# Wider squares, one of them on ScalarE, another load order and earlier softmax chains in a fused attention and channel-mix kernel

## The chip, the core and the metric

The kernel runs on one core of a Trainium2 chip. The metric is the device time of one execution in microseconds. TensorE (PE) multiplies matrices and writes to PSUM; VectorE (DVE) and ScalarE (ACT) do elementwise work; GpSimd (POOL) here mostly issues the DMAs that convert f32 to bf16 on the way; SyncE (SP) issues the other DMAs and the DMA transposes. Each engine works through its own list of instructions in order and waits on semaphores for the others.

## The reference

Two layers follow each other, for 4 batches of 6208 rows and 256 channels. The first is an attention over channels: a 256 x 256 matrix per batch, built from q and k normalised over the rows, goes through a softmax and multiplies v. The second mixes each row with the row before it and runs a two-matrix network with a squared relu and a gate.

```python
qn = q / (np.linalg.norm(q, axis=1, keepdims=True) + 1e-06)
kn = k / (np.linalg.norm(k, axis=1, keepdims=True) + 1e-06)
s = kn.transpose(0, 2, 1) @ qn / tau
a = softmax(s)                        # with the usual maximum subtracted
x = v @ a                             # [4, 6208, 256]
xk = mu_k * x + (1.0 - mu_k) * x_prev # x_prev: the row before, zeros in front
xr = mu_r * x + (1.0 - mu_r) * x_prev
k = np.maximum(xk @ w_k, 0.0)         # 1024 wide
out = sigmoid(xr @ w_r) * (k * k @ w_v)
```

## The kernel before

**Blocks.** A batch has 12 blocks of 512 rows and 64 left-over rows; the left-over rows of all batches make one last block. The main loop has an index i over blocks and eight steps j = 0 to 7 in each. At iteration i it holds three blocks in flight. For block i + 2, `x_half` makes x transposed from v (steps 0 and 2), `mix_delta` (step 3) and `mix` to xk (steps 4 and 5) follow on VectorE. For block i + 1, `up` makes one of eight 128-wide slices of the hidden layer in each step (PSUM tile kT_ps, three buffers), ScalarE applies the relu into kr, and `square` squares two slices at a time on VectorE into kk, a step after the second relu; the mix to xr runs at steps 0 and 2. For block i, `down` multiplies kk with w_v and xr with w_r (PSUM tile vr_ps, two buffers), `finish` takes the tanh on ScalarE and the last product on VectorE, and a DMA on SP stores the result. The last square of block i (`square(i, 7)`) is placed at step 0 of iteration i, and `down(i, 1)` at step 2 is the first that reads it.

**The next batch's covariance.** Batch 0's q and k are loaded, cast and multiplied ahead of the loop (VectorE casts, ScalarE squares). For batches 1 to 3 the covariance is cut into units, one per 128 rows: 1 for the left-over rows and 48 for the twelve groups of 512 rows. `unit` is put into the loop at the steps named in `slots`: three units in iteration 0, five in iteration 1, six in iterations 2 to 7, and three to five afterwards. Five early units are multiplied in iteration -1. A unit is two matmuls into s_ps (one buffer for batches 1 to 3). `feed` keeps ScalarE two units ahead with the squares of q and k, two units in one instruction, and `next_add` adds these squares to the accumulator acc on VectorE: at steps 1, 6 and 7, two steps or more after the square, and at every step once the batch's softmax chain is under way.

**The softmax chain.** When a batch's last unit is placed, `softmax_pieces` gives a list of pieces, and each following step of the loop takes one from its front: copy s_ps out (evac), fold acc, sum over partitions (norms), copy and take the root on GpSimd (roots, roots2), invert, spread the factors with a matmul, scale, exp, weigh. `None` is a step without a piece. `FOLD` is the length of the list at which fold is in front; it stays there while adds of that batch are open. The pieces norms and spread each take a PSUM buffer with the tag xT_ps, of which there are two, shared with x_half. weigh writes a_sb, which the first `x_half` of the next batch reads: x_half(12) at iteration 10, x_half(24) at 22, x_half(36) at 34.

**Loads.** GpSimd issues in program order v(0), w_k, q and k of the left-over rows, v(1), q and k of group 1, w_r, w_v, v(2), q and k of group 2; then v(i + 5) at step 0 of each iteration, and q and k up to three groups ahead of the unit in hand (`loads_upto`), into five buffers. v(0), v(1) and v(2) are transposed on TensorE, the others by DMA on SP, issued at step 5 of iteration i for block i + 4. The tile qk holds [128 partitions, 4 rows, q or k, 256 channels], so each row of q lands as 512 bytes between rows of k.

Of the kernel before, what the change touches and what calls it, by code (L numbers as in the profile page):

```python
# [10 lines left out]
F32 = mybir.dt.float32  # L11
BF16 = mybir.dt.bfloat16
AX = mybir.AxisListType.X
AF = mybir.ActivationFunctionType
OP = mybir.AluOpType
# [3 lines left out]
def kernel(  # L19
# [13 lines left out]
    nc = tc.nc  # L33
    B, N, C = q.shape
    D = C
    DF = moe_w_k.shape[1]
    P = 128
    M = 512
    S = M // P
    assert C == 256 and DF == 1024  # L40
    NB = N // M
    L = N - NB * M
# [3 lines left out]
    bounded = abs(inv_tau) < 32.0  # L46

    const = ctx.enter_context(tc.tile_pool(name="const", bufs=1))
    pq = ctx.enter_context(tc.tile_pool(name="pq", bufs=4))
    pn = ctx.enter_context(tc.tile_pool(name="pn", bufs=2))  # L50
    p2 = ctx.enter_context(tc.tile_pool(name="p2", bufs=3))
# [35 lines left out]
    sums = {}  # L87
# [5 lines left out]
    def sizes(b):  # L93
        return [1] + [S] * (NB - 1) + ([S // 2] * 2 if b == 0 else [S])

    def order(b):
        g = list(range(len(sizes(b))))
        return [1, 2, 0] + g[3:] if b == 0 else g

    def rows_of(b, g):  # L100
        return (P if g else L), sizes(b)[g]

    def qk_src(t, b, g):
        if g == 0:
            return t[b, NB * M:, :].rearrange("(p j) c -> p j c", j=1)
        r = P * sum(sizes(b)[1:g])
        n = sizes(b)[g]
        return t[b, r:r + P * n, :].rearrange("(p j) c -> p j c", p=P)

    def group_load(b, g):  # L110
        rows, n = rows_of(b, g)
        qk = pq.tile([P, S, 2, C], BF16, name="qk", tag="qk", bufs=5)
        groups[b, g] = (qk,)
        if b == 0:
            qk2 = pq.tile([P, S, 2, C], BF16, name="qk2", tag="qk2", bufs=4)
            groups[b, g] += (qk2,)
            t_f = []
            for i, t in enumerate((q, k)):
                f = pq.tile([P, S, C], F32, name=f"f{i}", tag=f"f{i}", bufs=6)
                nc.sync.dma_start(f[:rows, :n], qk_src(t, b, g))  # L120
                t_f.append(f)
            groups[b, g] += tuple(t_f)
        else:
            for i, t in enumerate((q, k)):
                nc.gpsimd.dma_start(qk[:rows, :n, i, :], qk_src(t, b, g))  # L125

    def group_cast(b, g):
        rows, n = rows_of(b, g)
        qk, qk2, *t_f = groups[b, g]
        for i in range(2):  # L130
            nc.vector.tensor_copy(qk[:rows, :n, i, :], t_f[i][:rows, :n])  # L131
        for i in range(2):
            nc.scalar.activation(qk2[:rows, :n, i, :], t_f[i][:rows, :n], AF.Square)  # L133

    def unit_square(b, g, s):

        rows, n = rows_of(b, g)
        if s % 2:
            return
        qk = groups[b, g][0]  # L140
        if n == 1:
            t = pq.tile([P, 1, 2 * C], BF16, name="sq", tag="sq1", bufs=2)
            sums[b, "left"] = t
        elif (g, s) == (1, 0):
            t = pn.tile([P, 2, 2 * C], F32, name="acc", tag="acc", bufs=2)
            sums[b] = t
        else:
            t = pq.tile([P, 2, 2 * C], F32, name="sq2", tag=f"f{s // 2}", bufs=6)
            adds.append((now[0] + 2, b, t))
        nc.scalar.activation(t[:rows], qk[:rows, s:s + min(n, 2)].rearrange("p s i c -> p s (i c)"), AF.Square)  # L150

    def next_add():
        _, b, t = adds.pop(0)
# [2 lines left out]
    def unit_matmul(b, g, s):  # L156
        rows, n = rows_of(b, g)
        t0 = g == order(b)[0] and s == 0
        te = g == len(sizes(b)) - 1 and s == n - 1
        if t0:  # L160

            cov[b] = (ps.tile([P, 2, C], F32, name="s_ps", tag="s_ps" if b else "vr_ps", bufs=1 if b else 2),
                      ps.tile([P, 2 * C], F32, name="ssq_ps", tag="vr_ps", bufs=2) if b == 0 else None)
        s_ps = cov[b][0] if b or g <= DIRECT else cov["s"]
        qk = groups[b, g][0]
        for ih in range(2):
            nc.tensor.matmul(s_ps[:, ih, :], qk[:rows, s, 1, ih * P:(ih + 1) * P],  # L167
                             qk[:rows, s, 0, :], start=t0 and ih == 0, stop=te,
                             skip_group_check=True)
        if s == n - 1 and b == 0:  # L170
            if g > DIRECT:
                norms_direct(g)
            else:
                group_norms(b, g)
# [23 lines left out]
    def softmax_pieces(b):  # L198

        s_ps, ssq_ps = cov.pop(b) if b else cov[b]  # L200
# [16 lines left out]
                                 start=i == 0, stop=False, skip_group_check=True)  # L217

        def fold():
            t = pq.tile([P, 2 * C], BF16, name="sq", tag="sq", bufs=1)  # L220
            nc.vector.tensor_tensor(t, sums[b][:, 0], sums[b][:, 1], op=OP.add)
            sums[b] = t

        def norms():
            bank[b] = ps.tile([P, 2 * C], F32, name="bank", tag="xT_ps", bufs=2)
            for t, rows in ((sums.pop((b, "left"))[:, 0], L), (sums.pop(b), P)):
                for i in range(4):
                    nc.tensor.matmul(bank[b][:, C + i:C + i + 1], t[:rows, i * P:(i + 1) * P], ones[:rows, 0:1],
                                     start=rows == L and i == 0, stop=rows == P, skip_group_check=True)
# [61 lines left out]
        if b == 0:  # L291
            return [copies, gather, roots, evac, invert, spread, halves]

        return [evac, None, fold, None, norms, roots, roots2, None, invert, None, spread, scale,
                None if bounded else top, exp, None, weigh]

# [1 line left out]
    NBLK = len(blocks)  # L300
    L1 = L + 1
    xl = const.tile([P, 2, B, L1], BF16, name="xl")
    st = {}

    def size(i):
        return M if i < NBLK - 1 else B * L

    def v_load(i):
        b, t = blocks[i]
        v_bf = p2.tile([P, S, C], BF16, name="v_bf", tag="v_bf", bufs=5)  # L310
        nc.gpsimd.dma_start(v_bf, v[b, t * M:(t + 1) * M, :].rearrange("(s p) c -> p s c", p=P))  # L311
        st[i, "v"] = v_bf
# [99 lines left out]
    def up(i, fh):  # L412
        m = size(i)
        if fh == 0:
            st[i, "kk"] = p2.tile([P, 8, M], BF16, name="kk", tag="kk", bufs=2)
        xk = st[i, "xk"]
        kT_ps = ps.tile([P, M], F32, name="kT_ps", tag="kT_ps", bufs=3)
        for dh in range(2):
            nc.tensor.matmul(kT_ps[:, :m], w_k_sb[:, dh, fh * P:(fh + 1) * P], xk[:, dh, :m],  # L419
                             start=dh == 0, stop=dh == 1)  # L420
        if fh % 2 == 0:
            st[i, "kr", fh // 2] = p2.tile([P, 2, M], BF16, name="kr", tag="kr", bufs=3)
        nc.scalar.activation(st[i, "kr", fh // 2][:, fh % 2, :m], kT_ps[:, :m], AF.Relu, scale=0.5 ** 0.5)  # L423

    def square(i, fh):
        m = size(i)
        if fh % 2:
            kr = st.pop((i, "kr", fh // 2))[:, :, :m]
            nc.vector.tensor_tensor(st[i, "kk"][:, fh - 1:fh + 1, :m], kr, kr, op=OP.mult)  # L429

    def down(i, j):

# [73 lines left out]
    for g in order(0):  # L506
        group_load(0, g)
        group_cast(0, g)
        if g == DIRECT + 1:
            copies, gather, roots, evac, invert, spread, halves = softmax_pieces(0)  # L510
# [29 lines left out]
            pos["ld"] += 1  # L540

    chain = []
    FOLD = 14
    holds = [0]

    def unit(ahead=2):
# [13 lines left out]
    def next_load():  # L560
        group_load(*loads.pop(0))
        pos["ld"] += 1

    nc.gpsimd.dma_start(w_k_sb, moe_w_k.rearrange("(ko ki) f -> ki ko f", ki=P))
    next_load()
    v_load(1)
    next_load()
    nc.gpsimd.dma_start(w_r_sb, moe_w_r.rearrange("(ko ki) d -> ki ko d", ki=P))
    nc.gpsimd.dma_start(w_v_sb, moe_w_v.rearrange("(fo fi) d -> fi fo d", fi=P))
    v_load(2)  # L570
    next_load()
    roots()
    evac()
    nc.scalar.activation(gate, ones[:, 0:1], AF.Exp)
# [13 lines left out]
    early = units[:S + 1]  # L588
# [4 lines left out]
    left = {}  # L593
    for i in range(-2, NBLK - 1):
        for j in range(8):
# [4 lines left out]
                    finish(i, j // 2 - 1)  # L600
            if j == 0 and 3 <= i + 5 < NBLK - 1:
                v_load(i + 5)
            if chain:
                piece = chain[0]
                if len(chain) == FOLD and any(e[1] == holds[0] for e in adds):
                    piece = None
                else:
                    chain.pop(0)
                if piece is not None:
                    piece()  # L610
# [11 lines left out]
            if i + 2 < NBLK:  # L622
                n = i + 2
# [14 lines left out]
            if i == -1 and j in (5, 6):  # L638
                for u in early[:2] if j == 5 else early[2:]:
                    unit_matmul(*u)  # L640
            if (i, j) in ((0, 1), (0, 5), (1, 3)):
                unit_square(*early[{(0, 1): 0, (0, 5): 1, (1, 3): 3}[i, j]])
            if i < 0:
                slots = ()
            elif i == 0:
                slots = (3, 5, 7)
            elif i == 1:
                slots = (1, 2, 4, 5, 7)
            elif i < 8:
                slots = (1, 2, 3, 4, 5, 7)  # L650
            else:
                slots = (3, 5, 7) if (i - 8) % NB == 0 else (1, 3, 4, 5, 7) if (i - 8) % NB < 3 else (1, 3, 5, 7)
# [47 lines left out]
```

## Time and profile before

| What | Value |
|---|---|
| time, median of 13 runs (lowest to highest) | 516.44 us (514.34 to 518.2) |
| the profiled execution's own time | 516.5 us |
| its span, first to last instruction | 514.7 us |
| busy, TensorE | 493.3 us (96%) |
| busy, VectorE | 457.2 us (89%) |
| busy, ScalarE | 431.4 us (84%) |
| busy, GpSimd | 104.7 us (20%) |
| mean granted TensorE clock | 0.996 |

A row of the group view gives source line, engine, operation and tiles, then busy time in all and the mean of one in ns, then the idle time of that engine just before such instructions and what ended it. Instructions on VectorE and ScalarE begin a little before the one ahead of them has ended, so the distance from start to start is shorter than the duration. Matmul durations overlap in the same way: a busy TensorE is not TensorE at its peak, and the distance between starts tells more. In the view of waits a row is: engine, tile and line that waited, what it waited for, us in total, how often, the longest.

### The profile page before, as it was taken

To read this page: it belongs to the slowest core of one execution; us is meant where nothing else is said; L and a number is where in the kernel's file an instruction comes from. 1 tells how busy PE (TensorE), PEld (TensorE's weight loads), DVE (VectorE), ACT (ScalarE), POOL (GpSimd) and SP (SyncE) were. 2 spreads that over 40 slices of the span, in tenths; PEclk is the share of its full clock that TensorE was granted. 3 is DMA by queue.
4 is the path that set the end of the run, shared out by engine and by line. 5 is a ranking of instruction groups with operands and counts; after the bars stand their busy time and mean duration, and the time that the engine had idled before them with its cause. 6 is when DMAs were issued, how large, how long until landed. Compare 5 with 4: busy or idle time off the path is not lost.

```text
span 514.7 us, 9504 instructions
## 1 busy us (share of the span) xinstructions
PE 493.3 (96%) x3509; PEld 332.6 (65%) x3509; DVE 457.2 (89%) x788; ACT 431.4 (84%) x858; POOL 104.7 (20%) x143
## 2 busy tenths in 40 slices
PE   4888899999999999999999999999999999999996
PEld 2453666666666667667666667667666666666665
DVE  4557799999999999999999999999989788888884
ACT  6877899988988889888988898898877887878884
POOL 0046242213252321311243231210031110000000
PEclk9989999999999999999999999999999999999999
DMA  8989999999979999979899999965269756424123
GB/s 320 419 287 188 192 169 193 210 188 177 175 117 213 181 163 189 145 128 191 129 148 180 191 176 171 172 120 128 62 107 178 133 119 120 110 71 115 42 83 102
DMA packets 143735, 83.72 MB, mean 163 GB/s; under 512 B 51717, under 2 KB 140105, under 8 KB 143689
## 3 DMA queue, kind: packets, MB, share of 16 engines
q0 software_dynamic: 65808, 33.01, 51.8%
q1 hardware_dynamic: 77712, 49.98, 40.9%
q8 instruction: 27, 0.44, 0.4%
q10 hardware_dynamic: 168, 0.13, 0.1%
q14 instruction: 20, 0.16, 0.1%
HBM read 78.71 MB, written 25.43 MB: 202 GB/s over the span
## 4 chain that ended last, share of the span: by engine, by line
PE 70%; DVE 14%; DMA 9%; ACT 3%; POOL 2%; issue 1%; SPq 0%; DVEq 0%; ACTq 0%; POOLq 0%
PE vr_ps L448 26%; PE kT_ps L419 25%; PE xT_ps L348 7%; PE vr_ps L444 6%; DMA f<-in_k_dram 5%; DVE acc L154 4%; PE s_ps L167 4%; DVE kk L429 3%; DMA v_bf<-in_v_dram 2%; DVE xk L404 2%; DMA vT<-v_bf 2%; DVE res L458 2%; ACT kr L423 1%; DVE delta L394 1%; DVE xr L404 1%
## 5 line engine op out<-in xcount | busy, mean ns | idle before, releaser
L423 ACT ACTIVATE kr<-kT_ps 128x512 bf16<-128x512 f32 (+1 forms) x392 | 233.9, 600 | 40.9 <-PE kT_ps L419 37.1
L448 PE MATMUL vr_ps<-w_v_sb,kk 128*128 128x256 bf16 x1536 | 231.7, 273 | 0.6 <-DVE kk L429 0.3
L419 PE MATMUL kT_ps<-xk,w_k_sb 128*128 128x512 bf16 (+1 forms) x784 | 231.0, 377 | 0.2 <-DVE xk L404 0.2
L448 PEld LDWEIGHTS <-kk 128*128 128x128 bf16 x1536 | 149.5, 98 | 60.2 <-DVE kk L429 3.0
L429 DVE TENSOR_TENSOR kk<-kr 128x1024 bf16<-128x1024 bf16 (+1 forms) x196 | 133.2, 679 | 4.3 <-ACT kr L423 3.3
L458 DVE SCALAR_TENSOR_TENSOR res<-res,vr_ps 128x256 f32<-128x256 f32 x192 | 79.8, 416 | 27.7 <-ACT res L457 27.4
L419 PEld LDWEIGHTS <-w_k_sb 128*128 128x128 bf16 x784 | 76.1, 98 | 28.4 <-issue 0.3
L154 DVE TENSOR_TENSOR acc<-acc,sq 128x1024 f32<-128x1024 f32 x69 | 84.0, 1217 | 0.0
L167 PE MATMUL s_ps<-qk 128*128 128x256 bf16 (+1 forms) x392 | 72.3, 285 | 6.7 <-DVE qk L131 6.7
L457 ACT ACTIVATE res<-vr_ps 128x256 f32<-128x256 f32 x192 | 75.4, 393 | 1.3 <-PE vr_ps L448 1.3
L150 ACT ACTIVATE sq<-qk 128x1024 f32<-128x1024 bf16 (+1 forms) x72 | 75.2, 1046 | 0.0
L350 ACT CAST xT<-xT_ps 128x512 bf16<-128x512 f32 x94 | 55.8, 593 | 22.9 <-PE xT_ps L348 22.6
L444 PE MATMUL vr_ps<-w_r_sb,xr 128*128 128x256 bf16 x384 | 73.2, 272 | 0.0
L404 DVE SCALAR_TENSOR_TENSOR xr<-delta,mu_t,xT 128x512 bf16<-128x512 bf16 x96 | 71.5, 745 | 0.0
L404 DVE SCALAR_TENSOR_TENSOR xk<-delta,mu_t,xT 128x512 bf16<-128x512 bf16 x96 | 71.4, 745 | 0.0
L444 PEld LDWEIGHTS <-xr 128*128 128x128 bf16 x384 | 37.5, 98 | 45.4 <-issue 1.4
L125 POOL DMA_DIRECT2D qk<-in_q_dram x39 | 28.7, 736 | 180.0 <-ACT kr L423 140.5
L348 PE MATMUL xT_ps<-vT,a_sb 128*128 128x512 bf16 x188 | 56.1, 379 | 3.7 <-DVE a_sb L273 2.2
L311 POOL DMA_DIRECT2D v_bf<-in_v_dram x48 | 37.2, 777 | 66.6 <-DMA vT<-v_bf 61.7
L167 PEld LDWEIGHTS <-qk 128*128 128x128 bf16 (+1 forms) x392 | 38.2, 101 | 18.6 <-DVE qk L131 10.4
L394 DVE TENSOR_TENSOR delta<-xT 128x1024 bf16<-128x1024 bf16 x48 | 32.9, 685 | 0.1
L133 ACT ACTIVATE qk<-f 128x1024 bf16<-128x1024 f32 (+2 forms) x28 | 26.0, 947 | 7.9 <-DMA f<-in_q_dram 4.2
(82 smaller groups left out, 165.5 us busy)
## 6 DMA issues: line engine op xcount, KB each, us to landing
out_dram<-res SPq DMA_DIRECT2D x47, 512.0 KB, 4.8
v_bf<-in_v_dram POOLq DMA_DIRECT2D x48, 256.0 KB, 7.7
qk<-in_q_dram POOLq DMA_DIRECT2D x36, 256.0 KB, 5.9
qk<-in_k_dram POOLq DMA_DIRECT2D x36, 256.0 KB, 8.6
f<-in_q_dram SPq DMA_DIRECT2D x11, 512.0 KB, 8.4
f<-in_k_dram SPq DMA_DIRECT2D x11, 512.0 KB, 9.4
vT<-v_bf SPq DMA_TRANSPOSE x45, 7.6
f<-in_q_dram SPq DMA_DIRECT2D x2, 256.0 KB, 9.5
```

The lines of the kernel that those rows point to most:

```text
L150: nc.scalar.activation(t[:rows], qk[:rows, s:s + min(n, 2)].rearrange("p s i c -> p s (i c)"), AF.Square)
L154: nc.vector.tensor_tensor(sums[b], sums[b], t, op=OP.add)
L167: nc.tensor.matmul(s_ps[:, ih, :], qk[:rows, s, 1, ih * P:(ih + 1) * P], qk[:rows, s, 0, :], start=t0 and ih == 0, stop=te, skip_group_che ...
L348: nc.tensor.matmul(xT_ps, a_sb[:, b, ih, dh * P:(dh + 1) * P], vT[:, :, ih, :], start=ih == 0, stop=ih == 1)
L404: nc.vector.scalar_tensor_tensor(o[:, dh], st[i, "d"][:, dh], mu[:, dh:dh + 1], st[i, "x"][:, dh, :M], op0=OP.mult, op1=OP.add)
L419: nc.tensor.matmul(kT_ps[:, :m], w_k_sb[:, dh, fh * P:(fh + 1) * P], xk[:, dh, :m], start=dh == 0, stop=dh == 1)
L423: nc.scalar.activation(st[i, "kr", fh // 2][:, fh % 2, :m], kT_ps[:, :m], AF.Relu, scale=0.5 ** 0.5)
L429: nc.vector.tensor_tensor(st[i, "kk"][:, fh - 1:fh + 1, :m], kr, kr, op=OP.mult)
L444: nc.tensor.matmul(vr_ps[:, D:], xr[:, dh, s * P:(s + 1) * P], w_r_sb[:, dh, :], start=dh == 0, stop=dh == 1)
L448: nc.tensor.matmul(vr_ps[:, :D], kk[:, fh, s * P:(s + 1) * P], w_v_sb[:, fh, :], start=fh == 0, stop=fh == 7)
L457: nc.scalar.activation(res[:, s], vr_ps[:, D:], AF.Tanh, scale=0.5)
L458: nc.vector.scalar_tensor_tensor(res[:, s], res[:, s], 1.0, vr_ps[:, :D], op0=OP.add, op1=OP.mult)
```

## The change

The change has five parts.

1. **Squares.** kr holds four slices (two buffers of four instead of three of two), and VectorE squares four slices with one instruction, after the relu of the fourth; the last block of left-over rows keeps pairs. For blocks 1 to 33 (`by_act`) slice 0 is squared on ScalarE right behind its relu, and VectorE's first instruction takes slices 1 to 3.
2. **The tile qk** becomes [128, q or k, 4 rows, 256], so four rows of q are one run of 2 KB; the squares, acc and fold follow this order.
3. **Loads.** v(1) goes ahead of the left-over rows' q and k, v(2) ahead of w_r and w_v, and group 2 follows v(3) in iteration -2, group 3 follows v(4) in iteration -1.
4. **Slots.** Iterations 0 and 1 have six units like 2 to 7, and the squares of the early units move to steps 0, 2 and 4 of iteration 0. Each batch's last unit thereby comes four units earlier.
5. **Chains.** The list has 19 steps instead of 16, with fold right behind evac and more empty steps in between.

```diff
-        qk = pq.tile([P, S, 2, C], BF16, name="qk", tag="qk", bufs=5)
+        qk = pq.tile([P, 2, S, C], BF16, name="qk", tag="qk", bufs=5)
...
-                nc.gpsimd.dma_start(qk[:rows, :n, i, :], qk_src(t, b, g))
+                nc.gpsimd.dma_start(qk[:rows, i, :n, :], qk_src(t, b, g))
...
-            nc.vector.tensor_copy(qk[:rows, :n, i, :], t_f[i][:rows, :n])
+            nc.vector.tensor_copy(qk[:rows, i, :n, :], t_f[i][:rows, :n])
...
-        nc.scalar.activation(t[:rows], qk[:rows, s:s + min(n, 2)].rearrange("p s i c -> p s (i c)"), AF.Square)
+        nc.scalar.activation(t[:rows], qk[:rows, :, s:s + min(n, 2)], AF.Square)
...
-            nc.tensor.matmul(s_ps[:, ih, :], qk[:rows, s, 1, ih * P:(ih + 1) * P],
-                             qk[:rows, s, 0, :], start=t0 and ih == 0, stop=te,
+            nc.tensor.matmul(s_ps[:, ih, :], qk[:rows, 1, s, ih * P:(ih + 1) * P],
+                             qk[:rows, 0, s, :], start=t0 and ih == 0, stop=te,
...
-        return [evac, None, fold, None, norms, roots, roots2, None, invert, None, spread, scale,
-                None if bounded else top, exp, None, weigh]
+        return [evac, fold, None, None, None, norms, roots, roots2, None, None, invert, None, None, spread,
+                scale, None if bounded else top, exp, None, weigh]
...
-        if fh % 2 == 0:
-            st[i, "kr", fh // 2] = p2.tile([P, 2, M], BF16, name="kr", tag="kr", bufs=3)
-        nc.scalar.activation(st[i, "kr", fh // 2][:, fh % 2, :m], kT_ps[:, :m], AF.Relu, scale=0.5 ** 0.5)
+        if fh % 4 == 0:
+            st[i, "kr", fh // 4] = p2.tile([P, 4, M], BF16, name="kr", tag="kr", bufs=2)
+        kr = st[i, "kr", fh // 4][:, fh % 4, :m]
+        nc.scalar.activation(kr, kT_ps[:, :m], AF.Relu, scale=0.5 ** 0.5)
+        if fh == 0 and by_act(i):
+            nc.scalar.activation(st[i, "kk"][:, 0, :m], kr, AF.Square)
+
+    def by_act(i):
+        return 1 <= i < 3 * NB - 2
 
     def square(i, fh):
         m = size(i)
-        if fh % 2:
-            kr = st.pop((i, "kr", fh // 2))[:, :, :m]
-            nc.vector.tensor_tensor(st[i, "kk"][:, fh - 1:fh + 1, :m], kr, kr, op=OP.mult)
+        n = 4 if i < NBLK - 1 else 2
+        if fh % n == n - 1:
+            lo = 1 if fh == 3 and by_act(i) else fh % 4 + 1 - n
+            kr = st[i, "kr", fh // 4][:, lo:fh % 4 + 1, :m]
+            nc.vector.tensor_tensor(st[i, "kk"][:, fh // 4 * 4 + lo:fh + 1, :m], kr, kr, op=OP.mult)
...
-    FOLD = 14
+    FOLD = 18
...
     nc.gpsimd.dma_start(w_k_sb, moe_w_k.rearrange("(ko ki) f -> ki ko f", ki=P))
-    next_load()
     v_load(1)
     next_load()
+    next_load()
+    v_load(2)
     nc.gpsimd.dma_start(w_r_sb, moe_w_r.rearrange("(ko ki) d -> ki ko d", ki=P))
     nc.gpsimd.dma_start(w_v_sb, moe_w_v.rearrange("(fo fi) d -> fi fo d", fi=P))
-    v_load(2)
-    next_load()
...
             if j == 0 and 3 <= i + 5 < NBLK - 1:
                 v_load(i + 5)
+                if i < 0:
+                    next_load()
...
-            if (i, j) in ((0, 1), (0, 5), (1, 3)):
-                unit_square(*early[{(0, 1): 0, (0, 5): 1, (1, 3): 3}[i, j]])
+            if (i, j) in ((0, 0), (0, 2), (0, 4)):
+                unit_square(*early[{(0, 0): 0, (0, 2): 1, (0, 4): 3}[i, j]])
             if i < 0:
                 slots = ()
-            elif i == 0:
-                slots = (3, 5, 7)
-            elif i == 1:
-                slots = (1, 2, 4, 5, 7)
             elif i < 8:
                 slots = (1, 2, 3, 4, 5, 7)
```

More of the change, by code (lines that the diff above doesn't have):

```diff
@@ L141, in unit_square @@
         if n == 1:
-            t = pq.tile([P, 1, 2 * C], BF16, name="sq", tag="sq1", bufs=2)
+            t = pq.tile([P, 2, 1, C], BF16, name="sq", tag="sq1", bufs=2)
             sums[b, "left"] = t
         elif (g, s) == (1, 0):
-            t = pn.tile([P, 2, 2 * C], F32, name="acc", tag="acc", bufs=2)
+            t = pn.tile([P, 2, 2, C], F32, name="acc", tag="acc", bufs=2)
             sums[b] = t
         else:
-            t = pq.tile([P, 2, 2 * C], F32, name="sq2", tag=f"f{s // 2}", bufs=6)
+            t = pq.tile([P, 2, 2, C], F32, name="sq2", tag=f"f{s // 2}", bufs=6)
             adds.append((now[0] + 2, b, t))
-        nc.scalar.activation(t[:rows], qk[:rows, s:s + min(n, 2)].rearrange("p s i c -> p s (i c)"), AF.Square)
+        nc.scalar.activation(t[:rows], qk[:rows, :, s:s + min(n, 2)], AF.Square)
     def next_add():
@@ L219, in fold @@
         def fold():
-            t = pq.tile([P, 2 * C], BF16, name="sq", tag="sq", bufs=1)
-            nc.vector.tensor_tensor(t, sums[b][:, 0], sums[b][:, 1], op=OP.add)
+            t = pq.tile([P, 2, C], BF16, name="sq", tag="sq", bufs=1)
+            nc.vector.tensor_tensor(t, sums[b][:, :, 0], sums[b][:, :, 1], op=OP.add)
             sums[b] = t
@@ L225, in norms @@
             bank[b] = ps.tile([P, 2 * C], F32, name="bank", tag="xT_ps", bufs=2)
-            for t, rows in ((sums.pop((b, "left"))[:, 0], L), (sums.pop(b), P)):
+            for t, rows in ((sums.pop((b, "left")).rearrange("p i s c -> p (i s c)"), L),
+                            (sums.pop(b).rearrange("p i c -> p (i c)"), P)):
                 for i in range(4):
```

## The prediction

> **What bounds the kernel now.** I read the busy table in equal stretches first, then the marks of one block, then the waits, then single rows. Columns of the stretches: window, length, busy us (and instructions) of PE, PEld, DVE, ACT, POOL, granted clock, DMA share, GB/s.
>
> ```profile
> 12.00:24.00 12.00, 10.63 (x73) 4.99 (x71) 6.69 (x10) 10.12 (x11) 0.00 (x0) 1.00 1.03 420
> 48.00:60.00 12.00, 10.68 (x75) 6.53 (x74) 10.08 (x16) 9.41 (x20) 5.58 (x8) 1.00 1.45 196
> 72.00:84.00 12.00, 12.00 (x89) 8.38 (x87) 12.00 (x20) 11.72 (x24) 6.09 (x9) 1.00 1.46 177
> 108.00:120.00 12.00, 11.88 (x83) 7.83 (x82) 12.00 (x20) 10.74 (x22) 3.36 (x5) 1.00 1.38 185
> 204.00:216.00 12.00, 12.00 (x88) 8.46 (x87) 11.79 (x19) 10.32 (x22) 2.27 (x4) 1.00 1.12 190
> 432.00:444.00 12.00, 12.00 (x85) 8.08 (x84) 9.97 (x18) 9.66 (x22) 0.75 (x1) 1.00 0.44 89
> ```
>
> ```profile
> 91.01 0.68 DVE L394 TENSOR_TENSOR delta<-xT 128x1024 bf16<-128x1024 bf16 x1
> 101.40 0.68 DVE L394 TENSOR_TENSOR delta<-xT 128x1024 bf16<-128x1024 bf16 x1
> 211.24 0.69 DVE L394 TENSOR_TENSOR delta<-xT 128x1024 bf16<-128x1024 bf16 x1
> 220.80 0.69 DVE L394 TENSOR_TENSOR delta<-xT 128x1024 bf16<-128x1024 bf16 x1
> ```
>
> One delta is made per block, so its starts give the period: 10.39 us where a block carries six covariance units, 9.56 with four, 8.69 with none (430 us on). A unit is two matmuls that start 0.109 us apart, 0.2175 us: 8.69 + 4 x 0.2175 = 9.56, so TensorE bounds the four-unit and the unit-free blocks. Six units would be 9.99; 10.39 is VectorE's, which there has no idle time. The waits show what else TensorE lost:
>
> ```profile
> PE xT_ps L348 <- DVE a_sb L273: 2.2, 3, 0.9
> PE xT_ps L348 <- DMA vT<-v_bf: 1.5, 1, 1.5
> PE vT_ps L327 <- DMA v_bf<-in_v_dram: 1.3, 1, 1.3
> ```
>
> Three softmax chains end late (from matmul start to matmul start the holes are 1.07, 1.07 and 0.54 us, 2.7 in all), and in the opening block 3's and block 2's v come late.
>
> **The change part by part**, against the profiled execution's 516.5 us (span 514.7, 1.8 around it); the median of the runs is 516.44.
>
> ```profile
> L423 ACT ACTIVATE kr<-kT_ps 128x512 bf16<-128x512 f32 x384 | 230.8, 605 | 39.8 <-PE kT_ps L419 35.9
> L429 DVE TENSOR_TENSOR kk<-kr 128x1024 bf16<-128x1024 bf16 x192 | 131.5, 685 | 4.3 <-ACT kr L423 3.3
> L429 DVE TENSOR_TENSOR kk<-kr 128x512 bf16<-128x512 bf16 x4 | 1.7, 419 | 0.0
> L154 DVE TENSOR_TENSOR acc<-acc,sq 128x1024 f32<-128x1024 f32 x69 | 84.0, 1217 | 0.0
> L150 ACT ACTIVATE sq<-qk 128x1024 f32<-128x1024 bf16 x69 | 73.3, 1065 | 0.0
> ```
>
> *Quads.* No row has 2048 columns. From the two kk rows 512 columns cost 266 ns: a quad is 685 + 2 x 266 = 1217, a triple 951. Upper end: 2 x 685 = 1370, nothing saved. I take 1217, nearest to both rows; the acc row moves the same bytes in 1217. VectorE now runs 1217 + 951 instead of 4 x 685; as each start overlaps the end before by 0.08 (kk starts 0.60 apart), two fewer instructions give back 0.16, and the block falls by 0.57 - 0.16 = 0.41 us: 10.39 to 9.98, level with TensorE's 9.99. I allow 0.06 for the tie: 10.05. Blocks 2 to 7 of the loop: 6 x 0.34 = 2.0 us saved. Everywhere else TensorE is the limit and a lighter VectorE is worth nothing; if TensorE were faster there it would be the cover that is gone.
>
> *One of eight on ScalarE.* No row squares 512 columns of 128 rows. Relu of 512 columns takes 605 ns with starts 0.49 apart, the 64-row square of 512 columns 621, half the sq row is 532: 532 to 621, and I take 605, or 0.49 by starts. In a six-unit block ScalarE needs, by starts, 8 x 0.49 relu, 2 x 0.49 xT, 4 x 0.27 tanh, 3 x 0.95 squares, 0.1: 8.9, with the new one 9.4 of 10. Hidden, though the tanh and xT copy queued behind it come up to 0.5 later; vr and xT have two buffers, and that slack is over 1 us. The Trainium skill, "ScalarE: Activation LUTs", section "Rules for kernel authors", would keep a multiply on VectorE. By it the block would fall by 0.15 alone and the six blocks give 0.9 instead of 2.0; the rows say ScalarE has the room, so I go by them.
>
> *Slots.* Iterations 0 and 1 carry six units instead of three and five, and the three early squares move into iteration 0. Four units leave the end: 4 x 0.2175 = 0.87 us saved there. In front ScalarE pays: iteration 0 held 10.1 us of it (eight relus, two copies, three tanh, four squares of 0.95, the 64-row one 0.5) against 8.8 of TensorE; now six squares and kk's, 12.5 against 9.4. The relus may lag by kT's three buffers and the tanh by vr's two, so TensorE leaves iteration 0 some 2.2 us after its own 9.4.
>
> *Loads.* In the opening the DMA queue is full at 196 GB/s, 1.34 us per 256 KB tile, in order: w_v lands at 39.7 + 10.8 = 50.5, v(2) at 51.8, q and k of group 2 and v(3) at 55.9, as the trace has it. An issue is 0.7 to 0.9 us of GpSimd, which is 20% busy. In the trace the tenth transfer, v(2), was not issued until w_k, the second, had landed (2.2 us): eight in flight. In the new order w_k lands at 42.4 as before, then v(1) 43.8, the leftover rows 44.1, group 1 46.8, v(2) 48.1, w_r 48.8, w_v 51.5, v(3) 52.8, group 2 55.5. The wait for w_k falls on w_v's issue (39.7 to about 43); its use, near 53.5, still has 2 us. v(2)'s 1.3 us wait goes, and v(3)'s transpose (8.9 us) is there by 62, before its use. Late next is group 2, wanted at 54 to 55: up to 1 us, partly under ScalarE's lag. Group 3 and later still run ahead, with SP's transposes and stores unmoved. Opening: iteration 0 starts 1.35 earlier (52.0), lasts 11.6, iteration 1 lasts 10.0: iteration 2 starts at 73.6 to 74.2, before it was 73.6. I take 0.3 us lost.
>
> *q and k apart.* Destination runs grow from 512 bytes to 2 KB. The queue wrote 196 GB/s of bf16, so it read 392 of f32; loads of 4-KB runs reached 420. At most 7% of these transfers, at least nothing: I take nothing. The engines' reads keep their inner 256 or 512 columns: nothing.
>
> *Chains.* Iteration 7 ends batch 1's units at slot 2; the 19 steps put weigh at iteration 9, step 5, instead of 7, some 2.4 us earlier against a hole of 1.07. Batches 2 and 3 finish a whole block earlier, so weigh comes six steps sooner. The three holes close: 2.7 us. Behind batch 1 also go 0.5 us of VectorE lag that TensorE met in iterations 8 and 9. New waits: the next batch's first unit follows three matmul groups (1 us) behind evac, which needs s_ps's single bank copied (0.58 us, behind the xT copy and a tanh): 0.5 us. Norms and spread of batch 1 now sit at step 0, so x_half at step 2 takes their bank after one VectorE copy or scale at step 1: 0 to 1, I take 0.5. Roots2's power (2.1 us on POOL, loads queue behind it) keeps three steps before invert. An add burst at steps 2 and 3 of iteration 7: 0.2.
>
> Sum: +0.3 - 2.0 - 0.87 - 2.7 - 0.5 + 0.5 + 0.5 + 0.2 = -4.6, so 511.9 us.
>
> **The rivals.** (1) VectorE and TensorE, level at 10, hold each other up: VectorE waits for a late xT copy, TensorE for kk, and the six-unit blocks stay near 10.3. For it: ScalarE was 11.7 of 12 busy at 72 to 84. Against: delta to kk to delta takes about 9 us. Price 1.5: 513.4.
>
> (2) The opening costs more: group 2 stops ScalarE and TensorE in order, and the squares pile up. Price 2 to 3: 514.4. The trace has no iteration with 12.5 us of ScalarE, so this end is open.
>
> (3) The other side: the later quad. In a four-unit block (198 us) the second pair's kk ends at 198.88; TensorE wants columns 4 and 5 of it at 199.29, columns 6 and 7 at 199.51. A quad started at the same time ends at 199.41. The pair it replaces at step 6 pulls its start 0.3 us forward, ScalarE's new square pushes it 0.1 back: about 0.1 us is left. If it is missed by more than 0.13 us in each of the 36 full blocks from iteration 11 on, the gain of 4.6 is gone; at 0.25 us it ends at 511.9 + 9 = 521; on the 20 four-unit blocks alone, 516.9. Against: the tail's margin is 1.3 us, so the second is the likelier.
>
> (4) The chain doesn't do what it says: fold is held by adds, weigh stays late, 2.7 us remain: 514.6.
>
> **How the numbers follow.** Likeliest 0.57 (own range 510.0 to 513.8), (1) 0.14, (2) 0.10, (3) 0.13, (4) 0.06. A measurement of this kernel tells about 0.2%, 1.03 us, from no change: 515.4 to 517.5. Faster takes the likeliest, (1) and most of (2) and (4): 0.81. Same: tails of (2), (3) and (4), 0.06. Slower: the rest of (3) and mishaps of (2), 0.13. The range 509.6 to 516.6 leaves out the worse half of (3), the extremes of (2), and a gain of more than 6.8 (group loads 7% faster, no new wait at all).
>
> **What would show it.** Starts of delta 10.0 to 10.1 us apart from 85 to 135 us; kk rows of 1217 and 951 ns, a kk row on ScalarE near 600; no wait of xT_ps for a_sb; v_bf gone from TensorE's waits, s_ps waiting for evac once; iteration 2 no more than 0.6 us later. Wrong would be: TensorE waiting for kk in block after block, delta over 9.6 us apart at 200 us, or iteration 0 beyond 13 us.

## The result: slower by 0.6%, where 0.9% faster was forecast

The changed kernel took 520.5 us, median of 11 runs, against 515.84 for the kernel before; the ratio is 1.0058, with a 95% interval of 1.0037 to 1.0079. Ratios here leave out executions over 1.5% above the fastest of their kernel (five of twelve of the changed kernel, 524.3 to 538.1 us, and three of six in run 2 below), which the medians contain, so the loss is 3.0 us by the ratio and 4.7 by the medians. The profiled execution took 523.0 us (span 521.2), the longest of those that the ratio counts; it shows the losses at a larger size.

VectorE did become lighter and ScalarE heavier. First part of the page after:

```profile
PE 494.8 (95%) x3509; PEld 332.8 (64%) x3509; DVE 441.8 (85%) x692; ACT 447.7 (86%) x891; POOL 88.7 (17%) x143
```

The groups by shape after (busy us in all, mean ns of one, then idle time ahead of them):

```profile
L438 DVE TENSOR_TENSOR kk<-kr 128x2048 bf16<-128x2048 bf16 x63 | 76.9, 1220 | 0.5 <-ACT kr L425 0.4
L438 DVE TENSOR_TENSOR kk<-kr 128x1536 bf16<-128x1536 bf16 x33 | 31.4, 951 | 0.4 <-ACT kr L425 0.4
L427 ACT ACTIVATE kk<-kr 128x512 bf16<-128x512 bf16 x33 | 20.8, 630 | 1.1
```

The starts of delta after (VectorE's timeline):

```profile
81.43 0.68 DVE L395 TENSOR_TENSOR delta<-xT 128x1024 bf16<-128x1024 bf16 x1
91.42 0.68 DVE L395 TENSOR_TENSOR delta<-xT 128x1024 bf16<-128x1024 bf16 x1
102.10 0.69 DVE L395 TENSOR_TENSOR delta<-xT 128x1024 bf16<-128x1024 bf16 x1
117.17 0.69 DVE L395 TENSOR_TENSOR delta<-xT 128x1024 bf16<-128x1024 bf16 x1
127.50 0.69 DVE L395 TENSOR_TENSOR delta<-xT 128x1024 bf16<-128x1024 bf16 x1
138.62 0.69 DVE L395 TENSOR_TENSOR delta<-xT 128x1024 bf16<-128x1024 bf16 x1
200.01 0.69 DVE L395 TENSOR_TENSOR delta<-xT 128x1024 bf16<-128x1024 bf16 x1
209.67 0.69 DVE L395 TENSOR_TENSOR delta<-xT 128x1024 bf16<-128x1024 bf16 x1
```

Where nothing interferes a six-unit block takes 9.99 us (81.43 to 91.42), as forecast. But the next ones take 10.68, 15.07, 10.33 and 11.12. The view of waits after names what TensorE lost (tile and line, releaser, us in total, times, longest):

```profile
PE xT_ps L349 <- DMA vT<-v_bf: 4.3, 3, 3.3
PE vr_ps L453 <- DVE res L467: 2.2, 3, 1.0
PE s_ps L167 <- ACT s_sb L255: 1.2, 1, 1.2
PE vr_ps L457 <- DVE xT L342: 1.0, 2, 0.7
```

The wait for a_sb is gone, as is the one for v_bf. In their place stand DMA transposes that are late (4.3 us, in blocks that had no such wait before), the residual in the opening and behind batch 1, and the copy of the covariance out of s_ps once. (In the last row the xT named is a short instruction that started beside the quad; TensorE started when the quad ended.)

To see where the difference lies, both profiles are cut at the same deltas (delta 0 is that of block 0; the differences are of start times):

| Stretch | before | after | difference |
|---|---|---|---|
| start to delta 0 | 43.78 | 44.58 | +0.80 |
| 0 to 3 (opening) | 26.44 | 26.86 | +0.42 |
| 3 to 8 (six units) | 51.97 | 56.06 | +4.09 |
| 8 to 13 (end of batch 1) | 51.10 | 53.17 | +2.07 |
| 13 to 21 (mostly four units) | 76.30 | 77.00 | +0.70 |
| 21 to 25 (end of batch 2) | 40.86 | 40.20 | -0.66 |
| 25 to 33 | 76.30 | 76.57 | +0.27 |
| 33 to 36 (end of batch 3) | 28.08 | 26.87 | -1.21 |
| 36 to 47 and the tail | 119.87 | 119.89 | 0 |

That is the 6.5 us between the two spans. The first row is not shown to be an effect of the change: delta 0 comes at 42.4 to 44.6 us in all the profiles of this document. Two stretches carry the loss: the six-unit blocks, which were to gain 2, and the end of batch 1.

In the first of them the transposes stand out. SP's timeline, the longest single one of after, and ahead of it the one of before nearest to it in time (start, duration on SP):

```profile
88.92 2.75 SPq L318 DMA_TRANSPOSE vT<-v_bf  x1
```

```profile
89.93 7.76 SPq L319 DMA_TRANSPOSE vT<-v_bf  x1
```

From issue to landing the seven transposes between 50 and 120 us took 11.8 us at the median before and 16.6 after (all 45 of the kernel: 7.6 and 5.8). And the wait costs more than itself. Stretches after (columns as in the prediction; the granted clock is the number ahead of the last two):

```profile
108.00:120.00 12.00, 8.98 (x52) 5.77 (x52) 7.11 (x11) 7.52 (x15) 1.06 (x2) 0.86 1.29 210
112.00:114.00 2.00, 2.00 (x10) 1.22 (x8) 1.45 (x2) 1.95 (x4) 0.00 (x0) 0.50 1.32 163
114.00:116.00 2.00, 2.00 (x11) 1.26 (x10) 0.77 (x2) 0.67 (x2) 0.00 (x0) 0.66 1.29 154
```

TensorE idles 3.3 us until 111.02, and then runs at a clock of 0.50 and 0.66 for two stretches of 2 us: another 1.7 us lost (2 x 0.50 + 2 x 0.34). With 3.32 of wait that makes the 5.1 us by which this block is over 9.99.

### The profile page after: what moved, and what is told of

Its sections match the earlier page's. It is cut to its first block, busy times and chain, and to the rows that moved or that the text cites. A ratio compares the mean times of both kernels' runs of the same rounds, so it can differ in the third digit from the quotient of the medians.

```text
span 521.2 us, 9375 instructions
## 1 busy us (share of the span) xinstructions
PE 494.8 (95%) x3509; PEld 332.8 (64%) x3509; DVE 441.8 (85%) x692; ACT 447.7 (86%) x891; POOL 88.7 (17%) x143
## 3 DMA queue, kind: packets, MB, share of 16 engines
q0 software_dynamic: 38160, 33.01, 44.5%
## 5 line engine op out<-in xcount | busy, mean ns | idle before, releaser
L438 DVE TENSOR_TENSOR kk<-kr 128x1536 bf16<-128x1536 bf16 (+2 forms) x100 | 109.9, 1099 | 0.9 <-ACT kr L425 0.9
L351 ACT CAST xT<-xT_ps 128x512 bf16<-128x512 f32 x94 | 55.5, 591 | 15.8 <-PE xT_ps L349 15.7
L125 POOL DMA_DIRECT2D qk<-in_q_dram x39 | 21.0, 539 | 192.4 <-ACT kr L425 111.8
L312 POOL DMA_DIRECT2D v_bf<-in_v_dram x48 | 37.5, 782 | 70.2 <-DMA vT<-v_bf 66.7
```

The source lines that it names most:

```text
L438: nc.vector.tensor_tensor(st[i, "kk"][:, fh // 4 * 4 + lo:fh + 1, :m], kr, kr, op=OP.mult)
```

## The experiments

The theory drawn from these two profiles (T): the tile with runs of 2 KB makes the transposes late, and that is the loss; without it the forecast holds. Its rivals: the opening (O), and the concentration of work on VectorE at the end of batch 1 (E). All were timed in five rounds beside the kernel before; ratios are to it, with 95% intervals.

**1. The change without the new tile.** Everything but part 2 of the change:

```diff
-        qk = pq.tile([P, 2, S, C], BF16, name="qk", tag="qk", bufs=5)
+        qk = pq.tile([P, S, 2, C], BF16, name="qk", tag="qk", bufs=5)
```

> The changed kernel with one part undone: q and k are interleaved in the tile again, 512-byte runs. Theory T (the 2-KB runs hold up the DMA transposes of v while the queue is full): transposes land within 9 to 13 us between 60 and 115 us, TensorE no longer waits for vT, and 5 to 6.5 us of the changed kernel's 523.0 us go: 516 to 518 us. Theory L (six units in each of the first iterations and the new load order ask for more than the queue moves, whatever the runs): vT is still late, 519 to 523 us.

517.63 us, 1.0016 [1.0006, 1.0027]. TensorE no longer waits for a transpose, and two of them on SP take

```profile
53.21 5.38 SPq L318 DMA_TRANSPOSE vT<-v_bf  x2
```

where the changed kernel has

```profile
52.20 7.62 SPq L319 DMA_TRANSPOSE vT<-v_bf  x2
```

So the tile costs 0.42% (2.2 us) by the ratios. But the rest of the change isn't faster than the kernel before: the tile is only a part of what was missed.

**2. The new tile alone,** on the kernel before (the inverse edit and nothing else).

> The kernel before with q and k apart in the tile, and nothing else. T: transposes land later than 13 us between 60 and 115 us, and some block waits for vT; 516 to 521 us against 515.8 before, with more scatter. L: vT as before, 515.3 to 516.3 us.

529.26 us, 1.0164 [1.0142, 1.0185]. Beside the old load order the price is larger than in the change, and falls on block 3:

```profile
PE xT_ps L349 <- DMA vT<-v_bf: 8.8, 1, 8.8
```

```profile
55.97 8.91 SPq L319 DMA_TRANSPOSE vT<-v_bf  x2
```

The kernel before had 1.5 us of this wait and 4.84 us on SP for the two. Delta 0 to 3 takes 36.98 us instead of 26.44; every later stretch is as before to 0.15 us, so the new order of the tile costs the engines nothing. From 75 us on the transposes take 1.6 to 1.9 us on SP, less than before's 2.8 to 3.5. So here the length of the runs costs at one place, the first DMA transposes behind the loads of the opening; in the changed kernel, whose loads come in another order, it costs later.

**3. Runs of 1 KB,** half way, on the kernel before:

```diff
-        qk = pq.tile([P, S, 2, C], BF16, name="qk", tag="qk", bufs=5)
+        qk = pq.tile([P, 2, 2, 2, C], BF16, name="qk", tag="qk", bufs=5)
...
+                nc.gpsimd.dma_start(qk[:rows, :n // 2, i, :, :], src.rearrange("p (a e) c -> p a e c", e=2))
```

> The kernel before with q and k in pairs of rows: runs of 1 KB, between the 512 bytes of before and the 2 KB of the second run. Theory T, each transfer waiting its turn behind longer pieces: block 3's wait for vT lies between 1.5 us and 8.9 us, 4 us give or take 2, and the time is 518 to 524 us. If there is a threshold instead of a share: as before (516 to 517.5) or as with 2 KB (527 to 531).

520.47 us, 1.0072 [1.0051, 1.0092].

```profile
PE xT_ps L356 <- DMA vT<-v_bf: 4.5, 1, 4.5
```

```profile
55.05 7.18 SPq L326 DMA_TRANSPOSE vT<-v_bf  x2
```

Runs of 512 bytes, 1 KB and 2 KB give waits of 1.5, 4.5 and 8.8 us, and 4.84, 7.18 and 8.91 us on SP. These three show no threshold: the longer the runs of the loads, the longer the first transposes beside them. With the runs the issue of such a load on GpSimd shortens as well (0.74, 0.70 and 0.54 us); which of the two holds the transposes up no run separates.

**4. The squares alone,** on the kernel before (part 1 of the change).

> The kernel before with the squares alone (quads on VectorE, one of eight slices on ScalarE). Both theories: delta 9.98 to 10.05 us apart in the six-unit blocks instead of 10.39, TensorE no wait in the four-unit ones, 513.5 to 514.5 us. If instead the later quad costs what rival 3 of the prediction says, delta over 9.6 us apart at 200 us and 516 us or more.

514.16 us, 0.9949 [0.9935, 0.9964]. Delta 3 to 8 takes 49.94 us instead of 51.97: 2.03 saved in five blocks (2.4 with the sixth, 8 to 9), so rival (1) of the prediction, blocks near 10.3, did not come. TensorE's wait for a_sb went from 2.2 us to

```profile
PE xT_ps L348 <- DVE a_sb L273: 0.7, 2, 0.3
```

with the softmax chain unchanged. But delta 13 to 21 and 25 to 33 each grow by 0.82.

**5. Squares and loads** (parts 1 and 3; old tile, slots and chain).

> The kernel before with the squares and the new load order, old tile, old slots, old chains. T: the waits for v(2) and v(3) in the opening go (2.8 us), of which 1 to 2 reach the end: 512 to 513.5 us. L: the new order alone brings waits for vT, 515 us or more.

513.05 us, 0.9934 [0.9917, 0.9952], the lowest ratio of all. Delta 0 to 3 takes 24.77 us instead of run 4's 27.01: the waits for v are gone. By the ratios the step from run 4 is within the noise.

**6. Squares, loads and slots,** with the old chain list. Against run 5:

```diff
-            if (i, j) in ((0, 1), (0, 5), (1, 3)):
-                unit_square(*early[{(0, 1): 0, (0, 5): 1, (1, 3): 3}[i, j]])
+            if (i, j) in ((0, 0), (0, 2), (0, 4)):
+                unit_square(*early[{(0, 0): 0, (0, 2): 1, (0, 4): 3}[i, j]])
...
-            elif i == 0:
-                slots = (3, 5, 7)
-            elif i == 1:
-                slots = (1, 2, 4, 5, 7)
```

> The squares, the new load order and the new opening slots, with the interleaved tile and the old list of chain steps. Theory O (the opening is what the new slots cost: ScalarE's squares and the wait for group 2): delta of block 3 comes 28 to 30 us after that of block 0, as in the changed kernel with the old tile (29.6) and not as with the old slots (24.8); 516.5 to 518 us. Theory C (the new chain is what costs): 513 to 514.5 us.

517.6 us, 1.0014 [1.0001, 1.0027]. With the slots all of run 5's gain is gone, whichever list the chain has: delta 0 to 3 takes 29.49 us (24.77 without), 8 to 13 takes 52.75 (50.43 without). The units of iteration 0 now want the second q/k group before it lands (first row, until 57.37 us); the other two rows stand at 134 and 139 us, at the end of batch 1, where the covariance's copy and the fold are late with the old list too:

```profile
PE s_ps L167 <- DMA qk<-in_k_dram: 2.6, 1, 2.6
PE s_ps L167 <- ACT s_sb L254: 1.2, 1, 1.2
PE bank L228 <- DVE sq L221: 0.8, 1, 0.8
```

Behind the first wait the granted clock is 0.74, 0.50 and 0.90 in three stretches of 2 us from 56 us on, some 1.7 us lost; behind run 1's wait of 2.79 us for the same group it stays at 1.00. Run 6 and run 1 differ in the chain list alone, and their ratios are equal within the noise (1.0014 and 1.0016): no gain of the list is shown, and the slots cost 0.80% against run 5. The chain list alone, with the old slots, wasn't tried: a list of 19 steps then ends after the block that needs a_sb.

**7. Quads without ScalarE's slice.** Against run 5:

```diff
     def by_act(i):
-        return 1 <= i < 3 * NB - 2
+        return False
```

> The squares and the new load order, but no slice on ScalarE: all quads on VectorE. By the sum of the rows a quad in place of the triple is 0.27 us more per block: delta 10.25 us apart in the six-unit blocks instead of 9.99, so 1.6 us over six blocks and with it 514 to 515 us against 513.05; in the four-unit blocks 9.56 to 9.62. If ScalarE's slice holds TensorE up there (9.61 on average in the runs with it, 9.56 before), this run is back at 9.56.

515.68 us, 0.9977 [0.9964, 0.999]. The six-unit period is 10.26 us, with the slice 9.99. The four-unit blocks are as long as with it (13 to 21: 77.02 against 77.12), so it isn't ScalarE that lengthens them.

**8. The units of iteration 7 a step later,** on run 1, to give ScalarE's copy of s_ps more time:

```diff
+            elif i == 7:
+                slots = (1, 2, 4, 5, 6, 7)
```

> The changed kernel with the old tile, and in iteration 7 the units at steps 1, 2, 4, 5, 6, 7 instead of 1, 2, 3, 4, 5, 7: the next batch's first unit comes a step later behind evac. If the copy out of the one s_ps buffer is what TensorE waited 1.19 us for, that wait is gone and block 8 to block 9 falls from 11.1 to 10.0 to 10.2; of this 0.5 to 1.1 us reach the end: 516.5 to 517.2 us against 517.6. If VectorE's adds are the limit there, the end stays at 517.6.

517.92 us, 1.0019 [1.0005, 1.0033]: the expectation missed. TensorE's wait for the copy fell from 1.19 to 0.20 us, and its wait for the residual behind it rose from 0.93 to 1.92; delta 8 to 13 is 53.16 as in run 1. TensorE's rows of run 1, then of this run:

```profile
132.51 0.38 PE L167 MATMUL s_ps<-qk 64*128 64x256 bf16 x2 [1.19 <-ACT s_sb L254]
137.50 0.38 PE L452 MATMUL vr_ps<-w_r_sb,xr 128*128 128x256 bf16 x2 [0.93 <-DVE res L466]
132.98 0.38 PE L167 MATMUL s_ps<-qk 64*128 64x256 bf16 x2 [0.20 <-ACT s_sb L254]
137.99 0.38 PE L452 MATMUL vr_ps<-w_r_sb,xr 128*128 128x256 bf16 x2 [1.92 <-DVE res L466]
```

VectorE has no hole in run 1's block 8 to 9 (window, length, PE, PEld, DVE, ACT and POOL busy):

```profile
121.90:133.00 11.10, 9.86 (x74) 6.80 (x74) 11.10 (x16) 10.75 (x22) 3.59 (x5) 1.00 1.02 196
```

**9. Two additions less.** Run 1 without the last two additions of batch 1's squares:

```diff
+        if b == 1 and b == holds[0] and len([e for e in adds if e[1] == b]) < 2:
+            return
         nc.vector.tensor_tensor(sums[b], sums[b], t, op=OP.add)
```

> The change with the interleaved tile (the kernel that took 517.63 us), less the last two additions of squares of batch 1 on VectorE (so the norms of batch 1 lack four of 48 token groups; all else is computed and nothing else is moved). In the kernel without this edit VectorE is busy without a hole from 121.9 to 140 us, with four additions of 1.21 us between the delta operations of blocks 8 and 9 where other blocks of six units have three, and one more plus the fold ahead of the square after it. Theory A (VectorE's run of additions and the fold, put by the earlier chain into the blocks where VectorE has no room, is the cost of the new chain of batch 1): block 8 to 9 goes from 11.12 to 9.99, 9 to 10 from 10.91 to 9.7 or 9.8, 2.2 in all, and 517.63 becomes 515.2 to 515.8. Rival B (TensorE's wait of 1.19 us for ScalarE's copy of the covariance out of its bank, and the norms' matmuls, set the length of these blocks): they keep 11.1 and 10.9 to within 0.3, and the time stays at 517.3 to 517.8.

516.27 us, 0.999 [0.9979, 1.0002]. Between the two theories: block 8 to 9 fell to 10.42 us, 9 to 10 to 10.74, 0.87 in all where 2.2 were expected. TensorE's wait for the copy kept its 1.19 us, its wait for the residual behind it went. So VectorE's load is one limit, and there is a second right behind it.

**10. Both.** Runs 8 and 9 together (four of 48 groups lack in the norms, as in run 9).

> The change with the interleaved tile (517.63 us), with both edits that were tried one by one: the units of iteration 7 a step later (alone: 517.92) and the last two additions of batch 1 left out (alone: 516.27, block 8 to 9 10.42 and TensorE's wait of 1.19 us for the evacuation still there; the norms lack four of 48 groups). Theory C (two limits lie one behind the other at the end of batch 1, VectorE's additions and the evacuation of the covariance; each alone keeps the block long): TensorE's waits between 128 and 145 us fall from 1.19 to 0.3 or less, blocks 8 to 13 take 51.2 to 51.6 us where they took 52.29 with the additions left out alone, and the time is 515.0 to 515.6. Rival D (the wait only moves on, as it did when the units alone were moved): blocks 8 to 13 stay at 52.1 or more and the time at 516.0 to 516.6.

515.41 us, 0.9976 [0.9964, 0.9989]. Theory C held: delta 8 to 13 is 51.30 us, and of the 1.19 there remains

```profile
PE s_ps L169 <- ACT s_sb L256: 0.2, 1, 0.2
```

Run 1 has 53.16 us there, with one edit 53.16, with the other 52.29, with both 51.30.

**11. The q/k group ahead of v.** Run 1 with

```diff
-                v_load(i + 5)
                 if i < 0:
                     next_load()
+                v_load(i + 5)
```

> The change with the interleaved tile (517.63 us), with the q/k groups of iterations -2 and -1 issued ahead of the loads of v(3) and v(4) of the same steps. Theory O (with six units in iteration 0, the second q/k group is wanted at 53 us and lands at 55 to 57, because it stands behind v(2), the weights and v(3)): it lands some 1.3 us earlier (256 KB at 196 GB/s), the wait of 2.79 us at 55.88 goes to 1.5 or less, and the time to 516.2 to 516.9. Rival R (the opening is set by ScalarE's squares, by which the additions to the residual are late, and not by the group): the residual waits of 1.08 and 0.40 grow by what the group's wait loses, 517.3 to 517.9. Rival V: the transposes of v(3), now later, take the wait over, 517.5 to 518.5.

516.9 us, 1.0007 [0.9992, 1.0021]. The wait for the group is 0.48 us and the waits for the residual did not grow, as O says; but a transpose is late now, as rival V says:

```profile
PE xT_ps L348 <- DMA vT<-v_bf: 1.6, 1, 1.6
```

The interval overlaps run 1's, so the sum is not shown to be a gain. The wait for this group also differs between profiles that share their loads up to there: 2.79, 1.73, 0.15 and 1.09 us in runs 1, 8, 9 and 10. So the 0.48 is not shown to be the edit's either.

**12 to 14. On run 5, towards a faster kernel:** weigh one step earlier; pairs for the second four slices from block 9 on; and both, with the second quad only in blocks 3 to 8.

```diff
-                None if bounded else top, exp, None, weigh]
+                None if bounded else top, exp, weigh]
...
-        n = 4 if i < NBLK - 1 else 2
+        n = 4 if i < NBLK - 1 and (fh < 4 or i <= 8) else 2
```

> Squares and load order of the change, nothing else (interleaved tile, old slots), and the last piece of the softmax chain one step earlier. Theory H (the 0.34 us that TensorE waits for the softmaxed matrix after batches 1 and 2 and the 0.40 us at the start of batch 3's run are the step too late): the holes go, 513.05 becomes 512.0 to 512.7. Rival: the weigh operations, one step earlier, stand ahead of a square on VectorE instead, the block there is late by as much, and the time stays at 513.

> Squares and load order of the change (interleaved tile, old slots), but from block 9 on, where VectorE has room, the second four steps are squared in pairs again. Theory Q (where TensorE sets the pace, the second quad ends after the transposes that stand ahead of its first matmul have run out, which is the 0.05 us by which a four-unit block is longer than with pairs): the four-unit blocks go from 9.61 back to 9.56 on the mean, over some 24 of them 1.2 us: 511.5 to 512.3. Rival: the 0.05 us is something else (the ScalarE share of the squaring, by the run without it not): blocks stay at 9.61 and the time at 513; and pairs cost VectorE 0.28 us a block more, which, if VectorE is the bound there after all, makes it 513.5 to 515.

> Both together: quads in all of the first fours, in the second fours only in blocks 3 to 8 (the six-unit blocks), pairs elsewhere; weigh one step earlier. Theories H and Q and that the two waits of 0.70 and 0.33 us for squares at 65 and 76 us in the opening are the second quad: 510.0 to 511.5. If only one of them holds: 511.5 to 512.7. If neither: 513.

512.38, 512.03 and 512.28 us, beside a kernel before that took 515.09 there: 0.9949 [0.9937, 0.9962], 0.9949 [0.9936, 0.9961] and 0.9952 [0.9939, 0.9965]. None beats run 5's 0.9934; the times in us, 1.6 lower in the kernel before as well, are not to be held against those in the expectations. With weigh earlier (run 12) the 0.34 us of wait for a_sb go, and 0.70 us for the quad behind weigh and two additions appear, after batch 1 and after batch 2; 8 to 13 takes 50.48 us (50.43):

```profile
156.00 0.61 PE L456 MATMUL vr_ps<-w_v_sb,kk 128*128 128x256 bf16 x4 [0.70 <-DVE xT L341]
273.25 0.61 PE L456 MATMUL vr_ps<-w_v_sb,kk 128*128 128x256 bf16 x4 [0.70 <-DVE xT L341]
```

With pairs the four-unit blocks do go back to 9.56 us, from VectorE's timeline of run 13:

```profile
177.97 0.69 DVE L394 TENSOR_TENSOR delta<-xT 128x1024 bf16<-128x1024 bf16 x1
187.52 0.69 DVE L394 TENSOR_TENSOR delta<-xT 128x1024 bf16<-128x1024 bf16 x1
197.08 0.69 DVE L394 TENSOR_TENSOR delta<-xT 128x1024 bf16<-128x1024 bf16 x1
```

and the wait for a_sb comes back:

```profile
PE xT_ps L348 <- DVE a_sb L273: 2.3, 3, 0.9
```

13 to 21 and 25 to 33 gain 0.54 and 0.52, the three ends of batches lose 0.34, 0.29 and 0.59: nothing remains. Run 14, with both, takes 76.87 us from 13 to 21, between run 5's 77.12 and run 13's 76.58, and loses 0.60 us in the opening.

## Why the prediction was wrong, step by step

*Quads* and *One of eight on ScalarE*: right. Rows of 1220 and 951 ns for 1217 and 951; 630 ns on ScalarE for 605, inside its bounds; a period of 9.99 us for 10.05; 2.4 us saved in the six blocks for 2.0. The Trainium skill, "ScalarE: Activation LUTs", section "Rules for kernel authors", would have kept the multiply on VectorE; run 7 measures what that would cost here: 51.28 us instead of 49.94 in the five blocks, 0.43% of the time by the ratios. The rule speaks of the cost of the operation, and here the engine that has room decides.

Rival (3), the later quad, came in a small size beside it. It put the margin at some 0.1 us in a four-unit block; with the quad every second one takes 9.66 us (200.01 to 209.67 above) and the others 9.56. Delta 13 to 21, eight blocks with the ends of that stretch, is 0.70 us longer after, and pairs in run 13 give 0.54 of run 5's 0.82 back. The prediction had priced a miss of 0.13 us and more in each of 36 blocks, or 0.25 in each of 20; it came with 0.10 in every second one.

*Loads*: right in direction. Run 5 gains 2.2 us on run 4 from delta 0 to 3, or 1.5 from the first instruction on, for 1.35; the 0.15% by the ratios is within the noise.

*Slots*, the front part: mis-sized. The prediction took 0.3 us lost for loads and slots together, so 1.65 for the slots alone. From the first instruction to delta 3 the kernel before and run 4 take 70.2 us, the five runs with the new loads and the old slots (5, 7, 12, 13, 14) 67.7 to 69.6, and with the new slots as well (the changed kernel, runs 1, 6, 8, 9, 10) 71.2 to 73.6: 1.0 to 3.4 us lost in sum (run 11, with its other order of loads, takes 70.4). Where TensorE waited for the second group, the group came at 55.9 to 57.4 us, near the 55.5 of the forecast, but run 1 wanted it at 53.1 and not at 54 to 55; the "up to 1 us" is nothing to 2.8, by the profile. Behind it TensorE waits some 2 us more for the residual and a quad (0.98, 0.79 and 0.38 us in the changed kernel, of which run 5 has 0.70 for a quad); whether ScalarE's squares make these late no run tests. This is rival (2), priced at 2 to 3 us. That the changed kernel's opening lost only 0.42 us from delta 0 to 3, close to the forecast, is luck of its profile: it has no wait for the group, and run 9, with the old tile, has almost none either. The 0.87 us at the end came: from delta 13 to 36 run 6 takes 220.94 us, run 5 222.12.

*q and k apart* failed: "at most 7% of these transfers, at least nothing: I take nothing". This bounds the cost by the transfers themselves, and they did land no later: from issue to landing q took 5.5 us at the median for 5.9 before, k 6.2 for 8.6. The loser is another transfer, the transposes of v (the profile counts its queue on the same 16 DMA engines), which the step didn't price: 6.1 us in the profiled execution (the six-unit stretch gave +4.09 instead of -2.03), of it 4.3 waiting and 1.7 a slower clock after it, and 2.2 us by the ratios with and without the tile. The trace of before showed the wait that had to be asked about: 1.5 us for vT, once, beside a full queue. The Trainium skill, "DMA: Bandwidth & Descriptors", section "Queues, rings and completion order", says that each DMA engine takes turns between its queues by the packet. Runs 3 and 2 agree with it in direction, the GpSimd queue's packets falling from 65808 to 47376 and 38160 while its bytes stay at 33.01 MB; the taking of turns itself no run shows.

*Chains* failed. The forecast was -2.7 - 0.5 + 0.5 + 0.5 + 0.2 = -2.0 us, and run 1 against run 6 shows nothing gained by the list, with the wait for a_sb gone in both. Two things are wrong in it. First, most of the holes weren't the chain's to close: the squares of run 4 closed the wait for a_sb from 2.2 to 0.7 us with the old chain, and pairs in run 13 opened it again. Against run 5 the changed kernel's 21 to 25 is 40.20 us to 40.14: nothing gained. Second, the end of batch 1 got worse, 53.17 us to run 5's 50.43, and 2.3 of these 2.7 us are there with the old list in run 6: they come with the slots, by which the units end in iteration 7. The "add burst ... 0.2" and the "0.5 us" for the copy were to be sums beside each other; they are two limits, one behind the other, at a place where VectorE has no room. Four additions of 1.21 us and then a fifth with the fold fall into blocks that take 9.99 us with three. Rival (4) had named the place, "fold is held by adds", but priced it as holes that stay, not as a new loss. Runs 8, 9 and 10 settle this for the new list: the step alone gives nothing back, the additions alone 0.87 us, both together 1.86. What remains in run 10 against run 5 is 0.87 us. TensorE has waits of 0.25 and 0.65 us there, at 157 and 161 us, in the block that carries weigh. The second is the wait that run 12 shows when weigh alone comes a step earlier, with the same order on VectorE: weigh, two additions, the quad. The cause of the first was not tested.

In ratios, each against the one ahead of it: squares -0.51%, loads -0.15%, slots +0.80%, chain list +0.02%, the tile +0.42%: +0.58%. In us that is -2.6, -0.8, +4.1, +0.1 and +2.2; the forecast had -2.0, -1.35, +0.8, -2.0 and nothing (the costs at the end of batch 1, which came with the slots, it held among those of the chain). The first two were right in direction; the slots were five times as dear, the chain's gain wasn't there, and the tile was not free.

## What to carry to other kernels

A transfer's layout is to be priced by what shares its DMA engines, and not only by its own speed: look for the DMA wait that is already there beside a full queue. And work that is brought forward is to be laid against the engine that is full at the new place, all of the pieces at once, since two limits one behind the other hide each other from single edits. A hole that one part of a change closes may not be booked again for another part.

## What the runs showed of the hardware

- The first DMA transposes behind the loads of the opening take longer on SP, the longer the runs that these loads (with conversion) write: 4.84, 7.18 and 8.91 us for two at 512 bytes, 1 KB and 2 KB.
- An idle TensorE can be dear for longer than it idles: after 3.3 us without work the granted clock was 0.50 over one stretch of 2 us and 0.66 over the next, 1.7 us of work lost. The length of the wait alone doesn't tell: after 2.63 us in run 6 the clock fell to 0.50 as well, after 2.79 us in run 1 it stayed at 1.00.
- A square of 2048 columns in bf16 (1220 ns) costs 1.28 times one of 1536 (951) and 1.78 times one of 1024 (685): the 266 ns per 512 columns of the shorter rows held up to 2048.
